# A second q,k pair projected early, the PV products by token halves, and a new placement of the fill work

## The chip, the core and the metric

The kernel runs on one core of one Trainium2 chip. The metric is the time of the program on the device in microseconds (us). Names: TensorE (PE in the profile) multiplies matrices, PEld loads its weights; VectorE (DVE), ScalarE (ACT) and GpSimd (POOL) do the rest; SyncE (SP) issues the weight loads.

## The reference, cut to what matters

```python
x = A_x                                   # [1, 2048, 1024], bf16
for _ in range(2):
    x = x + attention(layernorm(x)) @ wo  # 32 heads of 32, window 8, dilation 2
    x = x + mlp_over_tokens(layernorm(x)) # 2048 -> 3584 -> 2048, gelu between
```

The attention of a token looks at itself and at 7 earlier tokens, two apart. So even and odd tokens never meet in it: the kernel cuts the tokens into two classes of 1024 and the heads into two halves, which gives four quarters per layer.

## The kernel before

For a quarter, VectorE makes products T of q with shifted k; TensorE sums them over a head's 32 columns (the scores); VectorE and ScalarE make the softmax Pb. Pb has one row per head, but the products with V need it on the 32 partitions of each head. This is done by two trips through memory, here called the *spread*: 256 KB out, and 2 x 1 MB back, each value read many times.

```python
def spread(self, n):                      # after: nc.gpsimd.dma_start(out=pd, in_=Pb)
    for hf in range(2):                   # token halves
        pb = pbp.tile([P, 4, W, TB], BF16, name="pb", tag="pb")       # 1 MB, two buffers
        ...
        nc.gpsimd.dma_start(out=pb[:]..., in_=src)

def pv(self, n, dq):                      # one 128-column tile: both halves one after the other
    for hf in range(2):
        pr = tpl.tile([P, 4, W, TB], BF16, name="pr", tag="T")
        # pr = pb * shifted V (VectorE), then three sums into oT (VectorE)
```

TensorE has little to do in attention itself (the scores are 39.2 us of its 1273.7 busy in before). *Fill* work from other stages is woven between: the second class's layer norm (layer 0) or second MLP matmul (`gemm2_tile`, layer 1), the V projections of the second class, the output projection of the first class (`out0`), and first parts of the next MLP matmul (`partials`, `late`). Two of these fills load a residual and store a sum, all on GpSimd's queue, and all from one pool of four buffers:

```python
x2p = pool("x2p", 4)
def out_proj(at_, c, res, dst, h2, on_act):        # on_act: the fill
    fetch(); fetch()                               # xr = x2("xr"), loaded by nc.gpsimd.dma_start
    for i in range(NT):
        xr = xrs[i]; xn = x2("xn")
        ...                                        # matmuls, then VectorE: xn = ps + xr
        fetch()
        nc.gpsimd.dma_start(out=dst_v[i], in_=xn[:])
def gemm2_tile(c, i, w2t, src, dst, hT, ...):
    xs = x2("xs"); nc.gpsimd.dma_start(out=xs[:], in_=src[c][...])
    xo = x2("xo")
    ...                                            # matmuls, then VectorE: xo = ps + b2 + xs
    nc.gpsimd.dma_start(out=dst, in_=xo[:])
```

`weave` sets the order of the instructions when the program is built. It keeps two estimated clocks, one for TensorE and one for VectorE, with 9 us for the spread, and from where the first output projection opens it uses an even rule:

```python
def even(p, d):                 # PE and VectorE cost of a unit of the attention
    pe += p
    dve = max(dve, pe - AHEAD) + d
    while pe < dve and pull():  # pull = emit one unit of fill
        pass
    pe = max(pe, dve)
```

The emitted order matters because VectorE works through its instructions in that order in these traces: one that waits holds up those behind it.

## Time and profile before

| | before |
|---|---|
| time, median of 3 runs | 1326.76 us (1325.8 to 1327.54) |
| PE busy, of the span of 1324.1 us | 1273.7 us (96%) |
| VectorE busy | 687.2 us (52%) |
| spread, issue to landing of one MB | 10.0 us median, 6.8 to 14.7 |
| the same for a residual of 256 KB | 3.5 us median |

Part 2 of the page, the busy tenths and TensorE's granted clock in 40 slices of 33 us:

```profile
PE   8997999999999999999999999999799999999999
DVE  6679899979502323244796646667970033111111
PEclk9998999999999999999999999999899999999999
```

TensorE is full in the two MLP stages (209.0 us busy of the 210 from 360 to 570 us, 318.4 of the 320 from 990 to 1310 us). It falls behind in the two attention stages (40 to 356 us and 574 to 986 us), where VectorE is busiest (267 of 316 us and 288 of 412). Its longer waits in the whole run, nearly all of them there, were (line waited on, releaser, us in total, times, longest):

```profile
PE sc L435 <- DVE T L430: 14.5, 13, 4.2
PE ps L608 <- DVE oT L503: 10.6, 3, 6.9
PE ps L400 <- DMA wq<-in_A_wqkv_dram: 2.6, 2, 2.2
...
PE ps L667 <- DMA w<-in_B_w_dram: 2.0, 1, 2.0
```

So scores wait for T, the output projections wait for the attention's result oT, and a few weights come late. Several of these waits cost more than themselves, as half clock follows them in the records. The windows view (its columns: length, then PE, PEld, DVE, ACT and POOL busy with counts, granted clock, share of the DMA engines, GB/s) shows it for the wait for T at 104 to 119 us and, in the second line, for the 6.9 us wait for oT at the end of layer 1:

```profile
104.00:119.00 15.00, 7.84 (x42) 2.58 (x42) 13.78 (x11) 3.87 (x4) 0.00 (x0) 0.77 0.23 71
950.00:962.00 12.00, 6.06 (x19) 2.37 (x20) 11.20 (x17) 0.29 (x1) 0.56 (x1) 0.72 0.00 0
```

The granted clock is 0.50 from 110.1 to 116.9 us, and 0.50 from 953.2 to 960.0 us. All half-clock stretches of before, but for the last, are 3.4 or 6.8 us long. Shorter waits had one behind them too: 2.4 us in before (granted clock 0.51 from 219.3 to 222.8 us).

To see where time goes I use one figure of my own: the *lost time* up to a given amount of matmul work, which is the time at which that work was done less the work at full pace (0.216 us for each 128x512 matmul, as spaced in the trace, where 49 take 10.74 us, the last of them 0.38; 0.0555 us for each small score matmul, an estimate: in before, 16 of them take 1.05 us at 212.03 us where 8 take 0.62 at 207.92, which gives 0.054). The work is the same in all kernels, so differences of this figure are differences in time. It is read from one profiled run of each kernel, and runs of one kernel lie some 4 us apart, so a difference of 1 or 2 us in it says little.

### The profile page before, as it was taken

The numbers are of one execution on the slowest core, as the hardware profiler recorded it, in microseconds if no ns is written. First come the engines' busy times: TensorE is split into PE (matmuls) and PEld (weight loads), VectorE is DVE, ScalarE is ACT, GpSimd is POOL, SyncE is SP. The second block draws the span as 40 slices with busy tenths as digits, with TensorE's granted clock in tenths as the row PEclk, the third lists the DMA queues.
The fourth block names the chain that finished last, engine by engine and source line by source line (L and its number), as shares of the span: only waits on it lengthen the run. The fifth ranks groups of instructions, "written<-read, shape, count | busy, mean of one in ns | idle before, by whom it ended". The sixth has DMA issues, their size and how long they took to land. (4 is left out here: it accounts for less than half of the span.)

```text
span 1324.1 us, 15310 instructions
## 1 busy us (share of the span) xinstructions
PE 1273.7 (96%) x6163; PEld 576.4 (44%) x6284; DVE 687.2 (52%) x861; ACT 438.6 (33%) x740; POOL 95.2 (7%) x230
## 2 busy tenths in 40 slices
PE   8997999999999999999999999999799999999999
PEld 4343443443444444444444444444344444444444
DVE  6679899979502323244796646667970033111111
ACT  6843456532213420024424524575212244000000
POOL 3000002000100000000001010011020000000000
PEclk9998999999999999999999999999899999999999
DMA  9651536462532248862749772438253222334332
GB/s 256 143 135 53 131 90 189 148 155 72 159 87 73 75 138 215 216 170 89 168 138 244 198 194 56 103 106 235 65 163 84 75 85 72 117 96 137 118 117 60
DMA packets 239448, 173.00 MB, mean 131 GB/s; under 512 B 32208, under 2 KB 227152, under 8 KB 237328
## 3 DMA queue, kind: packets, MB, share of 16 engines
q1 hardware_dynamic: 224432, 116.67, 33.3%
q0 software_dynamic: 14368, 54.29, 14.7%
q8 instruction: 49, 0.80, 0.3%
q10 hardware_dynamic: 576, 1.05, 0.2%
q14 instruction: 23, 0.19, 0.0%
HBM read 146.81 MB, written 18.87 MB: 125 GB/s over the span
## 5 line engine op out<-in xcount | busy, mean ns | idle before, releaser
L641 PE MATMUL ps<-h,w 128*128 128x512 bf16 x1754 | 387.9, 379 | 5.6 <-ACT h L229 1.4
L667 PE MATMUL ps<-g,w 128*128 128x512 bf16 (+1 forms) x1781 | 387.2, 376 | 4.1 <-DMA w<-in_B_w_dram 2.0
L667 PEld LDWEIGHTS <-w 128*128 128x128 bf16 x1820 | 177.4, 98 | 213.0 <-issue 3.8
L641 PEld LDWEIGHTS <-w 128*128 128x128 bf16 x1792 | 175.1, 98 | 217.5 <-issue 6.5
L400 PE MATMUL ps<-hT,wq 128*128 128x512 bf16 (+1 forms) x1149 | 261.5, 380 | 6.1 <-DMA wq<-in_A_wqkv_dram 2.6
L672 DVE SCALAR_TENSOR_TENSOR xo<-ps,b_sb,xs 128x512 bf16<-128x512 f32 (+1 forms) x65 | 45.7, 738 | 257.3 <-PE ps L667 246.3
L400 PEld LDWEIGHTS <-wq 128*128 128x128 bf16 x1176 | 114.6, 100 | 148.0 <-issue 23.9
L430 DVE TENSOR_TENSOR T<-q,k 128x4096 bf16<-128x4096 bf16 x64 | 143.5, 2284 | 53.3 <-ACT q L404 45.3
L652 DVE TENSOR_TENSOR tmp<-ps,g 128x512 f32<-128x512 f32 x80 | 55.3, 692 | 205.3 <-PE ps L641 201.1
L501 DVE TENSOR_TENSOR pr<-pr 128x2048 bf16<-128x2048 bf16 (+1 forms) x128 | 120.0, 945 | 0.3
L608 PE MATMUL ps<-wo,oT 128*128 128x512 bf16 x374 | 91.1, 385 | 12.0 <-DVE oT L503 10.6
L407 ACT CAST k<-ps 128x1024 bf16<-128x1024 f32 x64 | 64.6, 1014 | 98.3 <-PE ps L400 88.6
L490 DVE TENSOR_TENSOR pr<-pb,g 128x2048 bf16<-128x2048 bf16 x64 | 77.0, 1215 | 30.8 <-DMA pb<-pd 21.2
L490 DVE TENSOR_TENSOR pr<-pb,v 128x2048 bf16<-128x2048 bf16 x64 | 76.2, 1215 | 20.8 <-DMA pb<-pd 14.3
L400 PE MATMUL ps<-hT,wv 128*128 128x512 bf16 x377 | 85.1, 379 | 1.2 <-DMA wv<-in_A_wqkv_dram 0.7
L653 ACT ACTIVATE g<-tmp,b_sb 128x512 bf16<-128x512 f32 x80 | 57.7, 721 | 82.1 <-DVE tmp L652 82.1
L647 ACT CAST g<-ps 128x512 bf16<-128x512 f32 x80 | 46.3, 585 | 75.4 <-PE ps L641 73.1
L191 ACT ACTIVATE ln<-mv,eps 128x1 f32<-128x1 f32 x37 | 10.9, 293 | 167.3 <-DVE mv L200 160.0
L608 PEld LDWEIGHTS <-oT 128*128 128x128 bf16 x384 | 37.5, 99 | 60.1 <-DVE oT L503 12.1
L400 PEld LDWEIGHTS <-wv 128*128 128x128 bf16 x384 | 43.0, 113 | 40.7 <-issue 1.3
L435 PE MATMUL sc<-T,sel 128*32 128x512 bf16 x512 | 39.2, 388 | 14.5 <-DVE T L430 14.5
L404 ACT CAST q<-ps 128x512 bf16<-128x512 f32 x64 | 37.0, 582 | 44.8 <-PE ps L400 42.2
(92 smaller groups left out, 615.2 us busy)
## 6 DMA issues: line engine op xcount, KB each, us to landing
w<-in_B_w_dram SPq DMA_DIRECT2D x96, 448.0 KB, 3.8
w<-in_B_w_dram SPq DMA_DIRECT2D x56, 512.0 KB, 4.8
wq<-in_A_wqkv_dram SPq DMA_DIRECT2D x40, 512.0 KB, 4.1
pb<-pd POOLq DMA_DIRECT2D x16, 1024.0 KB, 10.0
wo<-in_A_wo_dram SPq DMA_DIRECT2D x16, 512.0 KB, 3.9
xa<-xn POOLq DMA_DIRECT2D x32, 256.0 KB, 3.5
xs<-xa POOLq DMA_DIRECT2D x32, 256.0 KB, 3.6
wv<-in_A_wqkv_dram SPq DMA_DIRECT2D x12, 512.0 KB, 7.0
```

The costliest lines, as they stand in the source:

```text
L400: nc.tensor.matmul(ps[:, lo:hi], lhsT=cols, rhs=self.hT[c][hf][:, kt, lo:hi], start=(kt == 0), stop=(kt == KD - 1))
L407: nc.scalar.copy(out=window(buf, 0, PADK + hf * HT, [(KW + 1, 2), (1, HT)]), in_=ps[:].unsqueeze(1).to_broadcast([P, 2, HT]))
L430: nc.vector.tensor_tensor(out=T[:], in0=q[:].unsqueeze(1).to_broadcast([P, 4, SC]), in1=window(k, par, 2, [(2, 4), (1, SC)]), op=ALU.mult)
L490: nc.vector.tensor_tensor(out=pr[:, :, u, :], in0=pb[:, :, u, :], in1=window(v, par, 2 + hf * HT, [(TB, 4), (2, 4), (1, TB)]), op=ALU.mult)
L501: nc.vector.tensor_tensor(out=pr[:, :, 0:wd, :], in0=pr[:, :, 0:wd, :], in1=pr[:, :, wd:2 * wd, :], op=ALU.add)
L608: nc.tensor.matmul(ps[:], lhsT=at_.oT[c][kt][:, i * P:(i + 1) * P], rhs=wo_t[n][kt // 4][:, kt % 4, :], start=(kt == 0), stop=(kt == KD - 1))
L641: nc.tensor.matmul(ps[:], lhsT=wt[c][:, i, fl * P:(fl + 1) * P], rhs=h2[c][i // 4][:, i % 4, dc * 512:(dc + 1) * 512], start=(k == 0), sto ...
L647: nc.scalar.copy(out=gs, in_=ps[:])
L652: nc.vector.tensor_tensor(out=tmp[:], in0=ps[:], in1=gs, op=ALU.add)
L653: nc.scalar.activation(out=gs, in_=tmp[:], func=ACT.Gelu_apprx_tanh, bias=b1_sb[:, ft:ft + 1])
L667: nc.tensor.matmul(ps[:, 0:xc.stop - xc.start], lhsT=w2t[n][:, ft % HF, c::DIL], rhs=g[ft // GF][:, ft % GF, xc], start=(ft == 0), stop=(f ...
L672: nc.vector.scalar_tensor_tensor(out=xo[:, xc], in0=ps[:, 0:xc.stop - xc.start], scalar=b2_sb[:, i, c:c + 1], in1=xs[:, xc], op0=ALU.add, ...
```

## The change

The intent was to keep TensorE from waiting in attention, in three parts.

1. *Pair*: in layer 0, two more q,k tiles are projected early, their k's and part of their q's before attention starts, into buffers that are idle then, so VectorE has T's to make sooner. The first pair's V projections move behind them.
2. *Halves*: the PV products go by token halves: two tiles' first halves, then their second halves, so the second MB of the spread is needed later.
3. *Weave*: the fill is placed by a model of both engines with the spread's time in it (12 us for the first half, 6 more for the second), and this model now runs to the end of attention in place of the even rule.

```diff
@@ pair
+        def apart(self, c, dt):
+            return self.li == 0 and c == 0 and dt // 2 == 1
+        def q_of(self, c, dt):
+            return v_g[KD - 4 + dt % 2][:, 0, 0:SC] if self.apart(c, dt) else q_t[dt % 2][:]
...
@@ halves, in stream()
-                    if n > 0 and 2 * half >= done:
-                        yield from self.pv(n - 1, 2 * half)
+                    pv = n > 0 and half >= done
+                    if pv:
+                        yield from self.pv(n - 1, half, 0)
                     if half:
                         yield from self.softmax_back(n)
-                    if n > 0 and 2 * half + 1 >= done:
-                        yield from self.pv(n - 1, 2 * half + 1)
+                    if pv:
+                        yield from self.pv(n - 1, half, 1)
...
@@ weave
-        def even(p, d):
-            ...
+        def reach(t):
+            nonlocal pe
+            while pe < t - SLACK:
+                if not pull():
+                    pe = min([t] + [x for x in list(opened.values())[:1] if x > pe])
+            pe = max(pe, t)
...
-                if not blocked:
-                    even(after, cost)
-                    continue
-                dve = at_least(dve, waits) + cost
+                dve = max([dve] + [when.get(w, 0.0) for w in waits]) + cost
+                if then:
+                    reach(dve)
+                    pe += then
                 when.update((x, dve + lag) for x in sets)
-                pe += after
+                if list(opened)[:1] == ["out0"] and opened["out0"] < pe:
+                    due += cost
+                    if due > OUT0_GAP:
+                        due -= OUT0_GAP
+                        pull()
```

## The prediction

> **What bounds it now.** TensorE. The page gives PE 1273.7 us busy of 1324.1 (96%). The stretches without attention (350 to 575, 1000 to 1300 us) are solid in the stretch table (24.8 to 24.9 us in every 25), so the change can win only in the two attention stages. Back-to-back 128x512 matmuls start 0.216 us apart (49 in 10.74 us, chain of waits). Setting all matmuls at that pace against the time, I estimate that PE loses 31 us in attention of layer 0 (40 to 356 us) and 28 us in layer 1 (574 to 986); about 15 us of that are 0.3 us pauses around the 64 score groups, which stay. The rest, from the waits and timelines:
> - Layer 0, 104.8 to 119: score matmuls wait for VectorE (4.2 and 3.1 us), because VectorE idles earlier, 44.2 to 54.7 (no projection for the second q,k pair) and 82 to 87.6 (spread not landed). With the lowered clock after it (0.86 in 100 to 125 us): 10 us.
> - 219: 4 us; output projection of the second class, 312 to 356: 7 us.
> - Layer 1: 711 and 742, weights late, 6 us; 955.9, output projection waiting 6.9 us for oT, 9 us with the clock.
>
> [...] granted clock 0.86 to 0.93 in just the stretches with these waits.
>
> **What the change does.** By the instruction order, PE keeps its 6284 matmuls and VectorE its operations (T 2.28 us, product 1.22, sums 1.22/0.68/0.42). Only order and buffers change.
> 1. Second pair early: its T can start at about 45 us instead of 54.7. First softmax and spread then come about 6 us earlier (the next pair's projections now limit them). The spread takes 12 us either way.
> 2. Halves first: the second spread half, landing about 6 us after the first, is hidden (before: waits of 2.4 and 4.0 us at 93.6 and 712), and the output projection of the first tokens can start 8.7 us before the last sum.
> 3. Fill placement: more gemm fill between scores early in layer 1, V projections of the second class spread between T's, and fewer gemm1 partials ahead of the second output projection (19 us left over in layer 0, 31 us in layer 1).
>
> **On the critical path (estimates by summing durations along the new orders).** Layer 0: the wait at 105 shrinks from 10 to about 6.5; output projection of class 1 still waits about 6 us plus clock, but no wait follows it: gain 8 us. Layer 1, 711/742: loads further from the spread: gain 4. Layer 1 end: VectorE needs about 64 us from the last T to the last first-half oT, including 6 for the spread, while PE has only about 49 us of work there: PE idles about 11 us, not 7, after using less fill: loss 5.
>
> **Prediction:** 1326.8 - 7 = 1319.5 us, 80% range 1309 to 1328. Faster by over 2%: 0.05; within 2%: 0.93; slower by over 2%: 0.02.
>
> **In the profile after:** VectorE busy (687 us) unchanged; VectorE no longer idle at 45 to 54; class 1 output projection of layer 0 starting near 296 us (was 317); no weight wait near 700; in layer 1 a wait for oT of about 11 us, the longest, with clock under 0.9 there.
>
> **What would make it wrong:** the spread landing much sooner or later than 12 to 14 us; weight loads now colliding with it; VectorE waiting for TensorE's output tiles more or less than the order suggests.

The sum in it is 8 + 4 - 5 = 7 us. What the waits cost with the lowered clock is my estimate from the stretches of before (granted clock 0.86 from 100 to 125 us and from 950 to 975 us). The spread at 80.5 us of before landed its two halves, issued 0.5 us apart, 7.0 and 12.5 us after their issue, so 6 us apart; this is what that trace has for the 12 us and the 6 us in it.

## The result, and the profile after

After: 1326.8 us median of 4 runs (1323.72 to 1328.15); before, in the same rounds, 1327.15 us (4 runs). The ratio is 0.9993, 95% interval 0.997 to 1.0015. The class "within 2%" was right and the range held the time, which says little, as its upper end (1328) lay above the time of before. Of the 7 us gain nothing came that stands clear of the noise (the interval allows at most 4 us).

```profile
span 1326.4 us, 15310 instructions
...
PE   8999998999999999999997999999799999999999
DVE  6879998989102323234796734878950033111111
PEclk9998999999999999999998999999899999999999
```

TensorE's waits after:

```profile
PE sc L444 <- DVE T L439: 10.8, 4, 5.0
PE ps L622 <- DVE oT L506: 9.5, 3, 6.3
PE ps L681 <- DVE xo L686: 7.2, 1, 7.2
PE ps L622 <- DMA wo<-in_A_wo_dram: 3.4, 2, 2.9
PE ps L655 <- DVE xn L628: 2.1, 1, 2.1
```

The waits for T and late weights are down as intended, from 14.5 to 10.8 us and from 2.6 + 2.0 us to nothing. But there are new or longer lines: 7.2 us for an eviction of the gemm2 fill (`xo`; an *eviction* is the VectorE instruction that takes a finished sum out of a tile ps that TensorE wrote and so frees the tile; here TensorE waited those 7.2 us for one), 3.4 us for `wo` (1.1 before), 2.1 us for `xn`. The lost time, read at the same amounts of work, tells where:

| stretch (time before) | before | after | gain |
|---|---|---|---|
| start to 195 us | 30.1 | 25.5 | +4.6 |
| 195 to 219 us | 4.0 | 10.0 | -6.0 |
| 219 to 375 us (end of attention, layer 0) | 10.7 | 9.9 | +0.8 |
| 375 to 690 us | 5.4 | 3.7 | +1.7 |
| 690 to 746 us | 6.0 | 9.8 | -3.8 |
| 746 to 934 us | 7.7 | 7.5 | +0.2 |
| 934 to 973 us (end of attention, layer 1) | 9.0 | 8.9 | +0.1 |

The gain of the early start is there until 195 us and is given back right after; a second gain by 690 us is given back by 746. (The row to 219 us ends ahead of a half-clock stretch of before, 219.3 to 222.8 us, and includes that of after. Read to 225 us, before loses 5.6 and after 10.0, and the kernels are level.) The two places look alike. VectorE's timeline of after at the first (start, duration, instruction, and in brackets its idle time before and what ended it):

```profile
203.31 2.29 DVE L439 TENSOR_TENSOR T<-q,k 128x4096 bf16<-128x4096 bf16 x1
210.62 0.69 DVE L625 SCALAR_TENSOR_TENSOR xn<-ps,xr 128x512 bf16<-128x512 f32 x1 [5.03 <-DMA xa<-xn]
211.24 0.08 DVE L625 DVE_READ_ACCUMULATOR xn<-ps,xr 128x1 f32 x1
211.24 2.29 DVE L439 TENSOR_TENSOR T<-q,k 128x4096 bf16<-128x4096 bf16 x1
```

An eviction of the output projection sat 5 us until a *store* (xa<-xn, of two tiles before) had landed and given up its buffer. Behind it in the same engine stood the T that TensorE needed: TensorE waited 4.4 us for it, until 213.6, and then ran at half clock (0.51) until 217.0:

```profile
213.58 1.04 PE L444 MATMUL sc<-T,sel 128*32 128x512 bf16 x8 [4.44 <-DVE T L439]
```

The store had been issued right after the spread, as GpSimd's timeline shows:

```profile
196.51 1.03 POOL L482 DMA_DIRECT2D pb<-pd  x2 [5.28 <-issue]
197.52 0.60 POOL L608 DMA_DIRECT2D xr<-in_A_x_dram  x1
199.59 0.56 POOL L630 DMA_DIRECT2D xa<-xn  x1 [1.47 <-DVE xn L625]
```

It took 10.9 us to land, at 210.5 us, where such stores take 3.4 us in the median; the two halves of the spread had landed at 204.7 and 209.4 us (8.2 and 12.4 us). The second place, at 710 us:

```profile
702.94 0.73 DVE L686 SCALAR_TENSOR_TENSOR xo<-ps,b_sb,xs 128x512 bf16<-128x512 f32 x1
710.23 1.23 DVE L500 TENSOR_TENSOR pr<-pb,v 128x2048 bf16<-128x2048 bf16 x1 [6.56 <-DMA pb<-pd]
716.39 1.41 DVE L686 SCALAR_TENSOR_TENSOR xo<-ps,b_sb,xs 128x512 bf16<-128x512 f32 x2 [4.93 <-DMA xs<-xa]
717.72 2.35 DVE L500 TENSOR_TENSOR pr<-pb,v 128x2048 bf16<-128x2048 bf16 x2
```

Here VectorE first waits for the spread and then, with the next eviction, for the load of a residual (xs) that was issued at 704.77 us, 2 us behind the spread, and took 11.4 us. TensorE waited for that eviction: 7.2 us idle, and half clock (0.50) from 715.3 to 722.1 us, in part after it.

### The profile page after: what moved, and what is told of

The parts are those of the page before. It is cut to its first block, busy times and chain, and to the rows that moved or that the text cites. A ratio compares the mean times of both kernels' runs of the same rounds, so it can differ in the third digit from the quotient of the medians. Undisturbed runs are those within 1.5% of the kernel's fastest.

```text
span 1326.4 us, 15310 instructions
## 1 busy us (share of the span) xinstructions
PE 1275.1 (96%) x6164; PEld 577.1 (44%) x6284; DVE 683.5 (52%) x861; ACT 439.8 (33%) x740; POOL 95.7 (7%) x230
## 4 chain that ended last, share of the span: by engine, by line
PE 64%; DVE 6%; DMA 4%; issue 1%; ACT 0%; POOL 0%; DVEq 0%
PE ps L681 27%; PE ps L655 22%; PE ps L409 11%; PE ps L622 3%; DVE pr L500 2%; DVE pr L504 1%; PE sc L444 1%; DMA xs<-xa 1%; DMA wq<-in_A_wqkv_dram 1%; DMA pb<-pd 1%; DMA xa<-xn 1%; DMA hT<-hb 0%; DVE xn L628 0%; DVE T L439 0%; DVE xn L625 0%
## 5 line engine op out<-in xcount | busy, mean ns | idle before, releaser
L655 PEld LDWEIGHTS <-w 128*128 128x128 bf16 x1792 | 175.8, 98 | 217.0 <-issue 7.2
L409 PE MATMUL ps<-hT,wq 128*128 128x512 bf16 (+1 forms) x1084 | 241.7, 376 | 4.6 <-DMA hT<-hb 1.6
L439 DVE TENSOR_TENSOR T<-q,k 128x4096 bf16<-128x4096 bf16 x60 | 136.0, 2287 | 65.2 <-ACT q L413 55.5
L409 PEld LDWEIGHTS <-wq 128*128 128x128 bf16 x1112 | 108.8, 100 | 133.5 <-issue 13.6
L409 PE MATMUL ps<-hT,wv 128*128 128x512 bf16 x436 | 102.2, 384 | 0.9 <-issue 0.4
L416 ACT CAST k<-ps 128x1024 bf16<-128x1024 f32 x60 | 60.8, 1016 | 77.8 <-PE ps L409 76.5
L409 PEld LDWEIGHTS <-wv 128*128 128x128 bf16 x448 | 48.8, 112 | 51.8 <-issue 8.7
L192 ACT ACTIVATE ln<-mv,eps 128x1 f32<-128x1 f32 x37 | 10.9, 294 | 165.0 <-DVE mv L201 157.4
L622 PEld LDWEIGHTS <-oT 128*128 128x128 bf16 x384 | 37.2, 99 | 62.8 <-DVE oT L506 10.7
L416 ACT CAST g<-ps 128x1024 bf16<-128x1024 f32 x36 | 36.5, 1017 | 41.1 <-PE ps L409 41.1
```

The costliest lines, as they stand in the source:

```text
L409: nc.tensor.matmul(ps[:, lo:hi], lhsT=cols, rhs=self.hT[c][hf][:, kt, lo:hi], start=(kt == 0), stop=(kt == KD - 1))
L416: nc.scalar.copy(out=window(buf, 0, PADK + hf * HT, [(KW + 1, 2), (1, HT)]), in_=ps[:].unsqueeze(1).to_broadcast([P, 2, HT]))
L439: nc.vector.tensor_tensor(out=T[:], in0=q.unsqueeze(1).to_broadcast([P, 4, SC]), in1=window(k, par, 2, [(2, 4), (1, SC)]), op=ALU.mult)
L622: nc.tensor.matmul(ps[:], lhsT=at_.oT[c][kt][:, i * P:(i + 1) * P], rhs=wo_t[n][kt // 4][:, kt % 4, :], start=(kt == 0), stop=(kt == KD - 1))
L655: nc.tensor.matmul(ps[:], lhsT=wt[c][:, i, fl * P:(fl + 1) * P], rhs=h2[c][i // 4][:, i % 4, dc * 512:(dc + 1) * 512], start=(k == 0), sto ...
```

## The experiments

Eighteen kernels ran, four of them with a wrong result, each compared with before in its own rounds. Theories were formed as they went: A, the new fill placement gives back what the pair gains; B, VectorE's chain limits the stage whatever the order; then, for the late residuals, the queue that they share with the spread (A again, in the second set; the expectations call a queue a ring) or the shared DMA engines (C; in after, from 702 to 718 us, queue q0 with the spread takes 66.5% of the time of the 16 engines and q1 33.4%). From the third set on, D is the theory, formed from landings like the 10.9 us above, that whatever is requested from the DMA engines during a spread lands only with it, and that the change put such transfers ahead of T's and evictions; E to H are its rivals, as each expectation words them.

### 1. The parts of the change alone

Each part was taken out by restoring the text of before: `p_pair` is before plus the pair, `p_halves` before plus the halves, `p_weaveonly` before plus the weave, `p_noweave` the pair and the halves with the old weave.

```diff
 # p_noweave, against after: the old weave() text, and
-    PB_LAG = 12.0
-    OUT0_GAP = 7.0
+    PB_LAG = 9.0
+    AHEAD = 10.0
```

> Before with the second q,k pair early and nothing else. Theory A: faster than before by 3 to 5 us, the gain sits in layer 0 before 200 us and stays to the end, as layer 1 is the same code. Theory B: TensorE is 3 to 5 us ahead at 195 us and has lost it again at 360 us, end within 2 us of before.

> Before with the PV products by token halves and nothing else. Theory A: 0 to 3 us faster (waits for the second half of the spread of 2.4 and 4.0 us go, the output projections start earlier). Theory B: within 2 us of before.

> Before with the new fill placement alone: no second pair, no halves. Theory A: slower than before by 3 to 8 us, with a wait of 5 us or more of TensorE for an eviction of the gemm fill in layer 1 between 690 and 730 us. Theory B: within 2 us of before.

> The kernel after with the fill placement of before: the second q,k pair and the token halves stay, the new model of both engines goes. Theory A (the new fill placement gives back what the pair gains: evictions that TensorE needs now stand behind work of VectorE that waits for the spread): faster than before by 4 to 8 us (0.994 to 0.997 of before), because the 7.2 us wait for an eviction near 710 us and the output-projection waits near 195 to 215 us are not there, while the gain of 4.6 us up to 195 us stays. Theory B (attention is limited by VectorE's chain and the spread, so whatever is gained early is lost at the next wait, whatever the placement): within 2 us of before.

| kernel | median us | ratio to before (95%) |
|---|---|---|
| p_pair | 1318.87 | 0.9953 (0.9932 to 0.9974) |
| p_halves | 1318.42 | 0.9944 (0.9919 to 0.9968) |
| p_weaveonly | 1339.83 | 1.0113 (1.0088 to 1.0139) |
| p_noweave (pair and halves) | 1321.89 | 0.9979 (0.9955 to 1.0002) |
| after (all three) | 1326.8 | 0.9993 (0.997 to 1.0015) |

Pair and halves each give 6 to 7 us, more than I had given them, but together about 3, with an interval that reaches 1. So it is not only the weave that gives back: the gains collide without it. B falls for the parts alone, as p_pair and p_halves keep what they gain. A is too narrow: p_noweave gains less than it said and keeps an eviction wait of 7.6 us, and p_weaveonly is 15 us slower, not 3 to 8, for another reason than it said. Its eviction wait in that place is gone (1.9 us in all), and it waits for oT instead:

```profile
PE ps L622 <- DVE oT L513: 19.7, 5, 7.9
```

The weave with the pair alone, or with the halves alone, was not run. Lost time at seven marks (each from the one profiled run):

| lost time at (time in before) | 195 | 252 | 375 | 690 | 746 | 934 | 973 us |
|---|---|---|---|---|---|---|---|
| before | 30.1 | 37.2 | 44.8 | 50.2 | 56.2 | 63.9 | 72.9 |
| after | 25.5 | 36.3 | 45.4 | 49.1 | 58.9 | 66.4 | 75.3 |
| p_pair | 24.5 | 29.2 | 38.6 | 44.3 | 50.2 | 57.3 | 66.0 |
| p_halves | 22.5 | 29.0 | 40.7 | 46.2 | 57.4 | 64.8 | 64.8 |
| p_noweave | 30.3 | 43.0 | 44.5 | 49.5 | 60.5 | 68.1 | 68.1 |

The jump at 746 us is in each kernel with halves (11.2, 11.0 and 9.8 us, against about 6 in before and p_pair). The jump between 195 and 252 us is in the two with pair *and* halves (12.7 and 10.8, against 7.1 in before, 4.7 in p_pair and 6.5 in p_halves). And the last one, at the end of layer 1, is *absent* with halves under the old weave (0.0) and back with the new (8.9). The largest waits of TensorE in p_noweave:

```profile
PE ps L409 <- DMA wv<-in_A_wqkv_dram: 9.4, 1, 9.4
PE ps L409 <- DVE xo L682: 7.6, 1, 7.6
```

The first is V weights that were issued at 126 us, as a spread went out, and took 12.8 us to land; the second is the eviction of the gemm2 fill again. In p_pair, VectorE waits for the same store as in after, but behind the last T (at 200.2 us) instead of ahead of it, and TensorE does not notice:

```profile
205.47 0.69 DVE L623 SCALAR_TENSOR_TENSOR xn<-ps,xr 128x512 bf16<-128x512 f32 x1 [1.86 <-DMA xa<-xn]
```

### 2. The residuals on another queue

If the residuals are late because they stand behind the spread in one queue, another queue mends it. My assumption, which no trace had shown before this set, was that a 256 KB store in ScalarE's queue does not wait for GpSimd's 2 MB. The edit does part them: in q_after_res, from 196 to 214 us, the residuals are issued by ScalarE, and queue q10 moves 0.91 MB while q0 moves 2.10 MB, the size of the spread (in after q0 moved 3.26 MB there, and q10 nothing).

```diff
-                nc.gpsimd.dma_start(out=xrs[-1][:], in_=res[len(xrs) - 1])
+                (nc.scalar if on_act else nc.gpsimd).dma_start(out=xrs[-1][:], in_=res[len(xrs) - 1])
 # and so for the store of xn, the load of xs and the store of xo in the fills
```

> The kernel after with the residual loads and stores of the two fills (output projection of the first class, gemm2 of the second class) issued by ScalarE instead of GpSimd, so they no longer follow the 2 MB of the spread in one ring; order of every other engine unchanged. Theory A (they were late because they stood behind the spread in that ring): the store of xn and the load of xs land in 3 to 5 us instead of 9 to 11, VectorE's idle of 5.0 us at 206 and 4.9 us at 711 us shrinks under 2 us, TensorE's waits of 4.4 us (T, 213) and 7.2 us (eviction, 710) shrink under 2 us and the half clock after them goes: 1312 to 1318 us, 0.990 to 0.994 of before. Rival C (what makes them late is the load on the 16 shared engines, not the ring): they land as late as before, time within 3 us of after (1324 to 1330).

> Second pair and halves with the fill placement of before, and the residual traffic of the fills issued by ScalarE. Theory A: the 6.1 us idle of VectorE at 210 us and the eviction wait of 7.6 us near 726 us go with their half clock; the 9.4 us wait for V weights at 132 us stays: 1306 to 1313 us. Rival C: within 3 us of the same kernel without the edit (1319 to 1325).

> Before with the second pair early, and the residual traffic of the fills issued by ScalarE. Here no T stands behind a late residual in VectorE's order (its idle at 204 us was 1.9 us and cost TensorE nothing), so theory A expects little in layer 0 and 2 to 5 us in layer 1 around 700 to 750 us: 1313 to 1318 us. Rival C: 1317 to 1321.

> The kernel before with the residual traffic of the fills issued by ScalarE: the control for what the edit is worth without the change. Theory A: VectorE's idle of 3.2 us at 215 us and the T wait of 2.4 us with its half clock go, 3 to 6 us faster (1319 to 1323). Rival C: within 2 us of before.

Measured: q_after_res 1328.38 us (1.0024 of before), q_noweave_res 1327.79 (1.0022), q_pair_res 1340.68 (1.0109), q_before_res 1335.9 (1.0083). The landing times of the stores xa<-xn around 200 us, in after and then in q_after_res:

```profile
DMA to landing us min/median/max: 3.1/7.5/10.9
```

```profile
DMA to landing us min/median/max: 3.4/7.2/10.9
```

The same store takes 10.9 us on either queue, and the same two waits of TensorE stay (4.1 us for T at 213 us, 6.7 us for the eviction), as does VectorE's behind the store. In q_after_res:

```profile
DVE xn L625 <- DMA xa<-xn: 4.7, 1, 4.7
PE ps L681 <- DVE xo L686: 6.7, 1, 6.7
```

So the shared queue is not the cause of these two waits. In q_noweave_res VectorE's idle at 210 us only falls from 6.1 to 4.5 us; its eviction wait near 726 us does go (0.9 us at most), but TensorE waits 7.6 us for a `wq` near 650 us instead. Worse, the edit cost before 11 us and p_pair 22 us: in p_pair TensorE waited 11.5 us for a `wo` tile that was issued at 192 us and took 14.8 us to land (at most 5.2 us in p_pair, at the same place), and 7.8 us for `wq` in layer 1 (7.7 us in q_before_res too). Why those weights got slower by it was not settled.

### 3. Less to wait for: residuals in place

Instead of a faster transfer, one that nobody waits for: the sum is written over the residual. That frees one of four buffers per tile, so an eviction no longer needs the store of two tiles before, and residuals can be loaded a tile earlier, ahead of the spread.

```diff
-        fetch()
-        fetch()
+        for _ in range(3 if on_act else 2):
+            fetch()
...
-            xn = x2("xn")
+            xn = xr if on_act else x2("xn")
 # gemm2_tile as a fill: xo = xs, and xs of tile i + 1 is loaded at the start of tile i
```

> The kernel after with the two fills' residuals updated in place (xn written over xr, xo over xs), which frees a buffer per tile: the eviction no longer waits for the store of two tiles before, and each residual is loaded one tile earlier, before the spread. Theory D: VectorE's idle of 5.0 us at 206 and 4.9 us at 711 us shrinks under 1.5 us, TensorE's 4.4 us wait for T at 213 and its half clock go (about 6 us), the 7.2 us wait for the eviction at 710 shrinks by 4 to 5 us (the product ahead of it in VectorE's order still waits for the spread until 710): 1313 to 1320 us. Rival E: within 3 us of after.

> Second pair and halves with the fill placement of before, and the residuals in place. Theory D: VectorE's idle of 6.1 us at 210 us and TensorE's losses of about 11 us around 205 to 225 us go for the most part, the eviction wait of 7.6 us near 726 us shrinks under 4 us; the wait for V weights at 132 us stays: 1304 to 1313 us, faster than both kernels. Rival E: within 3 us of the same kernel without the edit (1319 to 1325).

> The kernel before with the fills' residuals in place: the control. Theory D (the change put T's and evictions behind residual transfers that the spread delays, and this gave its gain back): before gains less than after did (9 us), 2 to 5 us, so 1320 to 1323 us, and after in place is then faster than before in place by 4 to 7 us. Rival F (the in-place residuals are just a gain that any version has): 1314 to 1318 us, equal to after in place within 3 us, and the lost 7 us stay unexplained.

| kernel | median us | ratio to before (95%) |
|---|---|---|
| r_after_inplace | 1316.21 | 0.9927 (0.9911 to 0.9944) |
| r_noweave_inplace | 1316.6 | 0.9934 (0.9918 to 0.995) |
| s_before_inplace | 1329.01 | 1.0018 (1.0005 to 1.003) |

VectorE in r_after_inplace at the place that had the 5 us:

```profile
203.64 2.29 DVE L439 TENSOR_TENSOR T<-q,k 128x4096 bf16<-128x4096 bf16 x1
205.85 0.68 DVE L625 SCALAR_TENSOR_TENSOR xr<-ps,xr 128x512 bf16<-128x512 f32 x1
206.46 0.08 DVE L625 DVE_READ_ACCUMULATOR xr<-ps,xr 128x1 f32 x1
206.46 2.29 DVE L439 TENSOR_TENSOR T<-q,k 128x4096 bf16<-128x4096 bf16 x1
```

The idle is gone, and the second T comes at 206.5 instead of 211.2 us. TensorE's lost time between 195 and 219 us falls from 10.0 to 4.1 us, and at 690 to 746 us from 9.8 to 4.2; its wait for the eviction goes from 7.2 to 2.5 us. After in place is in the range forecast for it. The control is not: it was to gain 2 to 5 us and lost 2. So 1.0018 and 0.9927 put after in place 0.9% below before in place, about 12 us, where 4 to 7 were forecast. The kernel before gains 2 us near 219 by the edit (lost time 4.0 to 1.9) and loses more later, among others by a new wait for `h` from ScalarE, near 246 us:

```profile
PE ps L641 <- ACT h L229: 3.2, 1, 3.2
```

So the late residuals are not a loss that any version has; it is one that the change made. The edit both frees buffers and loads earlier; the two were not run apart.

In r_noweave_inplace the early part improves as expected (the 12.7 us become 6.3), but the eviction wait near 720 us stays at 6.7 us: there the evictions stand, in VectorE's order, behind 19 us of products that began at 702.8 us when the spread had landed, and an earlier residual does not help. Expected was 1304 to 1313 us; at 1316.6 it missed.

### 4. A smaller spread

This asks whether it is the spread's 2 MB that delays those transfers. Both of these give a wrong result. The first try kept one tile per half for the whole program and moved a quarter of the bytes:

```diff
-                pb = pbp.tile([P, 4, W, TB], BF16, name="pb", tag="pb")
+                pb = pb_keep[hf]
-... (1, 4 * W * TB)])
+... (1, W * TB)])
```

> WRONG RESULT ON PURPOSE. The kernel after with only the first quarter of each spread moved (0.5 MB instead of 2 MB per spread; the rest of the two tiles is filled once at the start), instruction order otherwise the same. Theory D (whatever is requested from the DMA engines while the 2 MB of a spread are moving lands only when the spread does, whichever ring it is on, and each placement of the fill puts some needed transfer there): the spread lands 6 to 8 us after Pb instead of 12 to 15, the store of xn at 200 us lands in 3 to 5 us instead of 10.9, TensorE's waits of 4.4 (213 us) and 7.2 us (710 us) go: 1296 to 1308 us. Rival E (the new order itself makes TensorE wait; VectorE's work is the limit in the attention stages): within 6 us of after (1320 to 1330).

> WRONG RESULT ON PURPOSE. The same cut of the spread in the kernel before. Theory D: before loses about 15 us to the spread (wait at 105 us, 3 us at 219, weights late at 711 and 742), so 1305 to 1315 us; and after with the same cut is then faster than before with it by about the 7 us that were predicted (4 to 12 us). Rival E: the two stay equal within 3 us.

Measured: 1355.98 us (1.0223) and 1339.98 us (1.0117). The edit was at fault. The program emits the next spread ahead of the last products of the quarter before; with rotating buffers those read the old tile, with a kept one they had to wait for the new spread (VectorE waited for it 64.9 us in all and 15.3 at the longest in r_after_quarter, 26.6 in all in after), and filling the tiles at the start kept VectorE busy for 6.9 us. These two say nothing on the question. The second try keeps the rotation and makes the tile smaller, and the product reads its one block four times, at the same 1.22 us:

```diff
-                pb = pbp.tile([P, 4, W, TB], BF16, name="pb", tag="pb")
+                pb = pbp.tile([P, 1, W, TB], BF16, name="pb", tag="pb")
...
-                    nc.vector.tensor_tensor(out=pr[:, :, u, :], in0=pb[:, :, u, :],
+                    nc.vector.tensor_tensor(out=pr[:, :, u, :], in0=pb[:, :, u, :].to_broadcast([P, 4, 4, TB]),
```

> WRONG RESULT ON PURPOSE. The kernel after with a spread of a quarter of the bytes: the two tiles hold one of four blocks, rotate as before, and the product reads that block four times; order and dependences unchanged. Theory D: spread lands about 5 us after its issue (median 11.9 before), the store of xn at 200 us lands in 3 to 5 us instead of 10.9, the load of xs at 704 us in 3 to 5 instead of 11.4, the T wait at 213 us and the eviction wait of 7.2 us at 710 us go: 1300 to 1312 us. Rival G (the residuals are late for another reason, e.g. GpSimd issues them late or the store to memory is slow): their landing stays over 8 us; time may still fall by the shorter spread, but the two waits stay.

> WRONG RESULT ON PURPOSE. The kernel before with the spread of a quarter of the bytes, as s_after_quarter2 did for after (19.4 us faster than before, about 19 faster than after). Theory D: before has less behind the spread, so it gains less, 6 to 14 us (1313 to 1321), and after is ahead of it by the 5 to 13 us that the change is worth without the collisions. Rival H (the shorter spread is worth the same to both): 1305 to 1310.

Measured: after with the small spread 1307.45 us (0.9848, 0.9835 to 0.9862), before with it 1302.26 us (0.9826, 0.9813 to 0.984). The stores around 200 us in s_after_quarter2:

```profile
DMA to landing us min/median/max: 2.6/3.4/4.2
```

The store that took 10.9 us now takes at most 4.2, the load of xs 3.9 to 6.2 instead of 11.4, and TensorE's wait for the eviction at 710 us is 0.3 us. So it is the bytes of the spread that delay the residuals; this part is shown. But I had expected the kernel before to gain less by it (1313 to 1321 us), and it gains as much or more, even beyond the rival's 1305 to 1310: with a short spread the change is worth nothing. TensorE's waits for T in t_before_quarter2, 14.5 us in before, are now

```profile
PE sc L435 <- DVE T L430: 8.3, 13, 2.0
```

I read this as: the change mostly moves *where* TensorE pays for the spread, in before at 105 us (the lost time there falls by 8 us with the small spread), in after at 213 and 710 us. This reading is argued, not tested by itself.

### 5. The end of the attention stages

The theory here is that after stops filling too early at the end of attention: by the instruction order, 232 partial gemm1 matmuls stand ahead of the second output projection in layer 0, where the even rule of p_noweave has 304 (176 against 256 in layer 1); TensorE then waits for oT (9.5 us in after) while partials are left. `s_hybrid` uses the new placement only until the first output projection opens and the even rule from there; `s_hybrid_inplace` has the residuals in place as well.

```diff
         for kind, *unit in lead:
             if kind == "open":
+                evened = evened or unit[0] == "out0"
...
+                if evened:
+                    even(then, cost)
+                    continue
                 dve = max([dve] + [when.get(w, 0.0) for w in waits]) + cost
```

> The same without the in-place residuals: 1306 to 1316 us if the tail is worth about 9 to 14 us by itself and the residual waits stay (VectorE's idle near 206 us, eviction wait of 5 us or more near 710 us); 1320 to 1328 if VectorE's chain is the limit.

> After with the residuals in place and the new fill placement only up to where the first output projection opens; from there on the even placement of before, which keeps 304 instead of 232 partial gemm1 matmuls (16 us) ahead of the second output projection. If the tail's waits (oT, 4.5 us at 297 and 7.4 us at 934 with half clock after) come from the model letting TensorE stop filling too early, they fall under 2 us each: 1298 to 1306 us, faster than both kernels by over 1.5%. If VectorE's chain is the limit in the attention stages, the same time is lost elsewhere: within 4 us of after in place (1312 to 1320).

| kernel | median us | ratio to before (95%) |
|---|---|---|
| s_hybrid | 1312.02 | 0.9889 (0.9875 to 0.9902) |
| s_hybrid_inplace | 1303.28 | 0.982 (0.9806 to 0.9833) |

TensorE's longest waits in s_hybrid_inplace; those for oT, 9.5 us in after, are not in its list any more:

```profile
PE sc L444 <- DVE T L439: 7.0, 5, 5.1
PE ps L622 <- DMA wo<-in_A_wo_dram: 3.7, 2, 3.1
PE ps L655 <- ACT h L230: 2.7, 4, 1.0
```

The lost time at the end of layer 1 is 0.0 in both, as in p_halves, where it was 8.9 in after. The two mends add up: from after, in-place is worth 0.7% and the even rule 1.0%, and both together 1.7%. s_hybrid_inplace beats both kernels, with a correct result.

### 6. One more order

The wait that is left at 100 us (5.1 us for T; after has 5.0 us there and a granted clock of 0.50 from 100.9 to 107.7 us) has the T's behind products that wait for the first spread. Moving the second half's products behind the next T's:

```diff
+                    late = lead is not None and n == 1
+                    if late and half:
+                        yield from self.pv(0, 0, 1)
+                        yield from v_proj(0, 1)
...
-                    if pv:
+                    if pv and not (late and half == 0):
                         yield from self.pv(n - 1, half, 1)
```

> The hybrid placement with residuals in place, and in the second quarter of layer 0 the products of the second token half (and the V projections that follow them) moved behind the T's of the next two pairs. The T's of that pair stand about 9 us earlier in VectorE's order, so TensorE's wait at 100 us (5.2 us) and its half clock go: 1294 to 1299 us if nothing later gives it back; within 3 us of 1303 if the later V projections or products cost the same.

Measured: 1315.07 us (0.9922), 12 us slower by the medians than without the move, 13 to 14 us by the ratios; both expectations missed. The lost time at 149 us (in before) is 21.7 instead of 24.0, so the wait became smaller, but 6.1 us more are lost from there to 252 us and 9.1 more to the end of the attention of layer 0 (its longest wait is 7.2 us for `h` of the output projection). I take it that the VectorE work put off came due later.

## Why the prediction was wrong

The sum was: layer 0 a gain of 8, layer 1 at 711 and 742 a gain of 4, the end of layer 1 a loss of 5. Measured in the two profiled runs: a loss of 0.6, a loss of 3.8 (beside 1.7 gained before it), and a gain of 0.1.

- **Layer 0, "output projection of class 1 still waits about 6 us plus clock, but no wait follows it: gain 8 us".** This is the first step that failed. The early part was right in direction: T's from 49.6 us (45 predicted, 54.7 before), the loss of 10 us at 105 us down to 8 (6.5 predicted), 4.6 us ahead at 195 us. The output projection began at 301 us, not 296. But the sum reaches 8 us only if the 4 us listed at 219 us go as well (3.5 at 105 us and 1 at the output projection make 4.5), and there more was lost, not less: a wait came *ahead* of the output projection, at 213 us, which I had not in the sum. T stood behind an eviction that waits for a store, 10.9 us long under the spread, and 10.0 us were lost between 195 and 219 us. I had counted on the order and on durations of the operations, and on each wait for DMA only where the spread or weights were awaited. Residuals in place took this wait away (10.0 to 4.1 us lost).
- **Layer 1, "loads further from the spread: gain 4".** Weights were no longer late, as predicted, but a residual load was what fell into the spread now, and with it the eviction: 9.8 us lost where before lost 6.0. In place: 4.2. This term failed by the same step: the transfer that would be late was the wrong one.
- **Layer 1 end, "PE idles about 11 us, not 7, after using less fill: loss 5".** The direction of the fill was right (less is used), the size wrong: the wait was 6.3 us. What I missed is that the halves alone would have cleared this loss (0.0 in p_halves), so the placement cost about 9 us there, not 5, hidden in an unchanged total.
- **"VectorE busy (687 us) unchanged"**: 683.5 us. **"No weight wait near 700"**: right. **"VectorE no longer idle at 45 to 54"**: right in the main, as its first T is at 49.6. **"A wait for oT of about 11 us, the longest"**: 6.3 us, and the longest was the 7.2 us for the eviction.
- The pair and the halves are worth more than I gave them (6 and 7 us alone); their sum does not add up. That both move fill into the same few microseconds of spread is my guess, not shown.

The prediction named colliding transfers as a risk, but of weights. It was the residuals: small, and usually back in 3.4 us. Left open: why pair and halves together put V weights into the spread (9.4 us in p_noweave) and what share of the remaining 51 us of lost time could still be had; and what in the DMA engines holds a small transfer for as long as the spread lasts (10.9 us for the store), as no run shows it.

## What to carry to other kernels

Before moving work on an engine that works through its instructions in order, as VectorE does in these traces (the T at 211 us stood behind an eviction that waited 5.03 us), list for each instruction in the new place what it waits for, *including the buffer that it writes*: a store that must land before a buffer is free is a wait like that for a load, and under the big broadcast here it took three times its usual time (10.9 against 3.4 us). Prefer taking such waits away (in place, earlier loads) to issuing them elsewhere: a different queue brought nothing here (10.9 us for the store on either). And when two changes are each worth half a per cent alone and little together, look for a resource that both lean on; here it may be the spread.
